# Sinkhorn-sorted attention with a maxout layer: values of items 2 and 3 sorted as a row pair, a hand-written order of scores and sorts, and item 4's keys and queries loaded into the values' raw buffer

## The chip, the cores and the metric

The kernel runs on one core of a Trainium2 chip. The metric is device time in microseconds (us) of one execution; the profile takes one execution apart. Engines: PE (TensorE matmul) and PEld (its weight loads), DVE (VectorE), ACT (ScalarE), POOL (GpSimd, which here issues the loads) and SP (SyncE, which issues output DMAs and DMA transposes).

## The reference, cut to what matters

Four items (B = 4), 8 heads, 768 positions in 8 blocks of 96, head size 64. Each head's 8 x 8 sort matrix is normalised five times, and mixes the blocks of keys and values; attention then stays within a block. The result goes through a maxout layer.

```python
P = sort_net
for _ in range(5):
    P = exp(P - max(P)); P = P / sum(P, -1); P = P / sum(P, -2)
k_sorted = einsum('bhij,bhjcd->bhicd', P, k_blocks)
v_sorted = einsum('bhij,bhjcd->bhicd', P, v_blocks)
attn = softmax(q_blocks @ k_sorted.T / sqrt(64))          # per block, 96 x 96
x = (attn @ v_sorted) as [B * S, H * D] = [3072, 512]
out = maximum(x @ w1, x @ w2) @ w_out                     # 512 -> 1024 -> 512
```

The kernel takes max(a, b) as relu(a - b) + b, so it needs w1 - w2 (`w_difference`) and the product w2 @ w_out (`w_product`, from `w2_transposes`).

## The kernel before, in words

The items are called 1 to 4 here; in the code they are b = 0 to 3. All matrix operands are bf16, converted from f32 by the loads.

**Stages.** A prelude computes the sort matrices and item 1's attention. Then comes `for b in range(B)`: loop 1 (b = 0) does the layer of item 1 and the attention of item 2 between its parts, loop 2 the layer of item 2 and the attention of item 3, loop 3 that of items 3 and 4, and loop 4 only the layer of item 4. A loop's layer is a list `units`: eight `moe_h` (four hidden-column tiles for each half of the tokens, eight matmuls each), in loop 1 then four `w_product`, then twelve `moe_out` parts (six 128-token tiles, two parts of six matmuls each). Loop 1's first two `moe_h` are done in the prelude. After each unit some attention steps are emitted.

**Attention steps of an item.** `sort_k` (three calls of 32 matmuls) mixes keys; `sort_v` (four calls of 16) or `sort_v_pair` (eight calls of 16, for two items at once) mixes values; `q_transposes` (two halves) turns queries; `scores` (eight, SC[u]) multiplies and takes the exponential on ACT; `values` (eight, VA[u]) multiplies by the sorted values and normalises on DVE with a reciprocal and a product; `x_transposes` (four, TR[t]) turns the result, on PE for item 1 and by DMA transposes from SP's queue for the others. Queries of items 1 and 2 are turned on PE, those of items 3 and 4 by `pair_q` (two DVE copies) and a DMA transpose on SP.

**Which half of the array.** Values lie in `v_raw`, 128 partitions: rows 0 to 63 for one item (heads x blocks), rows 64 to 127 for another. `turn_v` reorders them into `v_dc`. A sort of values contracts over 64 rows: `sort_v` uses one half of PE's rows, `sort_v_pair` puts one item on each half by turns. Before, item 1 is in the first half, item 2 in the second, and items 3 and 4 share the buffer as a pair. `block_diagonals` builds the sort matrices' block-diagonal operands from the `selections`.

**What sets the order.** Each engine runs its instructions in program order (`manual_schedule`). Steps are placed in two ways before the change: `tail`, a dictionary from a unit's number to steps, and `steps`, a list that is spread evenly over the units from unit `lo` on:

```python
steps += group(*SC[0:2]) + VA[0:1] + group(*SC[2:4]) + VA[1:2] + group(VA[2], TR[0])
steps += group(*SC[4:6]) + VA[3:4] + group(VA[4], TR[1]) + group(*SC[6:8]) + VA[5:6]
...
want = -(-len(steps) * sum(cost[lo : n + 1]) // total)
```

So scores come in pairs. Copies out of PSUM (`evac`) go to ACT or DVE by `pick`, which compares two running counts of work, `load`; `elapse` lowers them. PSUM holds four tiles of 128 x 1024 f32 (`ps_f32`, `ps_bf16`); an `out_ps` tile is held over four `moe_out` parts.

**Loads.** All go through POOL's queue, in order: `load_k` in three pieces, `load_v` in two (item 1: three), `load_q` in one (item 1: four). Raw keys have two buffers, raw queries one (`q_raw`), raw values the one `v_raw`, so a load waits until the buffer's last reader is done. `keep_streaming` puts matmuls of zeros on PE in the prelude.

Of the kernel before, what the change touches and what calls it, by code (L numbers as in the profile page):

```python
# [16 lines left out]
def kernel(  # L17
# [114 lines left out]
    def load_q(b, by_pair=False):  # L132
        t = qpool.tile([128, H, R * D], BF16, tag="q_raw", name="q_raw", bufs=1)
        src = q[b].rearrange("h (p r) d -> p h (r d)", r=R)
        for hs in [slice(hp, H, HP) for hp in range(HP)] if by_pair else [slice(0, H)]:
            nc.gpsimd.dma_start(out=t[:, hs], in_=src[:, hs])  # L136
        q_raw[b] = t
# [7 lines left out]
    def load_k(b):  # L145
        k_raw[b] = kpool.tile([128, HB * D], BF16, tag="k_raw", name="k_raw")
        n = HB * D // NCH
        for ci in range(NCH):
            nc.gpsimd.dma_start(
                out=k_raw[b][:, ci * n : (ci + 1) * n],  # L150
                in_=k_src[b, :, ci * n : (ci + 1) * n],
            )

    def load_v(b, c0=0, pieces=2):
        r0 = (b % 2) * 64
        n = (BLK - c0) * D // pieces
        for m in range(pieces):
            nc.gpsimd.dma_start(
                out=v_raw[r0 : r0 + 64, c0 * D + m * n : c0 * D + (m + 1) * n],
                in_=v_src[b, :, c0 * D + m * n : c0 * D + (m + 1) * n],  # L160
            )
# [18 lines left out]
    load_v(0, 0, 3)  # L180
# [24 lines left out]
    load_v(1)  # L205
# [48 lines left out]
    maskJ = const.tile([128, 6, NB], FP32, tag="maskJ", name="maskJ")  # L254
# [26 lines left out]
    def selections(b):  # L281
        src = ident[0:G, b * 8 : b * 8 + 8]
        if b % 2 == 0:
            sel_v[b] = const.tile([G, 16, NB], BF16, tag=f"sel_v{b}", name="sel_v")
            nc.vector.tensor_copy(
                out=sel_v[b], in_=ident[0:G, b * 8 : b * 8 + 16].to_broadcast([G, 16, NB])
            )
        sel_k[b] = const.tile([G, 8, 16], BF16, tag=f"sel_k{b}", name="sel_k")
        nc.vector.tensor_copy(out=sel_k[b], in_=src.to_broadcast([G, 8, 16]))
# [3 lines left out]
    def block_diagonals(kinds, m0=0):  # L293
# [3 lines left out]
        for c, (m, b) in enumerate(kinds):  # L297
            sel = (
                sel_k[b].rearrange("g h w -> g (h w)")
                if m  # L300
                else sel_v[b].rearrange("g h j -> g (h j)")
            )
            nc.tensor.matmul(
                pe[:, c * 64 : c * 64 + 64],
                sel,
                p_bf.rearrange("p i j -> p (i j)"),
                start=True,
                stop=True,
            )
# [9 lines left out]
        for c, (m, b) in reversed(list(enumerate(kinds))):  # L319
            bd = const.tile([128, 8, NB], BF16, tag=f"bd{m}{b}", name="bd")  # L320
            nc.vector.tensor_tensor(
                out=bd,
                in0=maskM[:, m].to_broadcast([128, 8, NB]),
                in1=pt[:, c].to_broadcast([128, NB, 8]).transpose([0, 2, 1]),
                op=ALU.mult,
            )
            if m:
                bd_k[b] = bd.rearrange("p m i -> p (m i)")
            else:
                bd_v[b] = bd_v[b + 1] = bd.rearrange("p m i -> p (m i)")  # L330
# [18 lines left out]
    def q_transposes(b, half, eng=None):  # L349
# [11 lines left out]
        if b == 0:  # L361
            nc.tensor.matmul(
                ps[:, 0:128], fill[:, 0:128], ident, is_transpose=True, start=True, stop=True
            )
# [44 lines left out]
    def sort_v(b, t, n=0, eng=None):  # L409
# [3 lines left out]
        for m in range(16):  # L413
# [10 lines left out]
            ps[0:BLK].rearrange("p (d m) -> p m d", m=64),  # L424
            1024,
# [240 lines left out]
    keep_streaming(ps_f32("fill_ps"), 88 * 138, most=138)  # L666
# [15 lines left out]
    sort_k(0, 0, 2048, "A")  # L682
# [7 lines left out]
    SC[0]()  # L690
    SC[1]()
    q_transposes(0, 1, "D")
    SC[4]()
    VA[0]()
    scores(0, 2, 1024)
    VA[1]()
    SC[3]()
    values(0, 2, 1024)
    x_transposes(0, 0, "A")
    values(0, 3, 512)  # L700
# [3 lines left out]
    VA[4]()  # L704
    SC[6]()
    moe_h(0, 0, 0, "A", (1, 3))
    SC[7]()
    VA[5]()
    moe_h(0, 0, 1, "A")
    x_transposes(0, 2, "A")  # L710
    VA[6]()
    w_difference(2)
    VA[7]()
    w2_transposes(0, "D")()
    w_difference(3)
    for b in range(1, B):
        selections(b)
    for c, n, m in [(2, 1, 0), (3, 3, 1)]:
# [9 lines left out]
    def load_rest():  # L728
        load_q(1)
        load_k(2)  # L730

    tail = {
        2: [TR[3], lambda: w2_transposes(1, "A")(), load_rest],
        4: [lambda: turn(second, 0)],
        5: [lambda: block_diagonals([(0, 2), (1, 1), (1, 2), (1, 3)], 2)],
        6: [lambda: turn(second, 24), lambda: turn(second, 48)],
        7: [lambda: turn(second, 72)],
        8: [lambda t=t: sort_k(1, t) for t in range(3)],
        9: [lambda: load_v(2), lambda: load_v(3), lambda: load_k(3)],
        14: [lambda: load_q(2)],  # L740
        18: [lambda: pair_q(2, 0), lambda: pair_q(2, 1), lambda: load_q(3)],
    }
    for b in range(B):
# [20 lines left out]
        steps, lo = [], 0  # L764
        if b < B - 1:
            qs = [lambda half=half: q_transposes(b + 1, half) for half in range(2)]
            ks = [lambda t=t, b=b: sort_k(b + 1, t) for t in range(3)]
            SC, VA, TR = att(b + 1)

            def group(*fs):  # L770
                return [lambda: [f() for f in fs]]

            if b == 0:
                lo = 9
                vs = [lambda t=t: sort_v(1, t) for t in range(4)]
                for m, c in enumerate((0, 24, 48, 72)):
                    VA[m + 1 : m + 2] = group(VA[m + 1], lambda c=c: turn(both, c))
                steps = group(*vs[0:2]) + group(vs[2], qs[0]) + group(vs[3], qs[1])
            elif b == 1:
                vs = [lambda t=t: sort_v_pair(2, t) for t in range(8)]  # L780
                tail[0] = qs
                tail[10] = [lambda: pair_q(3, 0), lambda: pair_q(3, 1)]
                steps = group(*ks) + group(*vs[0:2]) + group(*vs[2:4]) + group(*vs[4:6])
                steps += group(*vs[6:8])
            else:
                tail[0] = qs
                lo = 4
                steps = group(*ks)
            steps += group(*SC[0:2]) + VA[0:1] + group(*SC[2:4]) + VA[1:2] + group(VA[2], TR[0])
            steps += group(*SC[4:6]) + VA[3:4] + group(VA[4], TR[1]) + group(*SC[6:8]) + VA[5:6]  # L790
            steps += group(VA[6], TR[2]) + group(VA[7], TR[3])
        done = 0
        for n, unit in enumerate(units):
            elapse(100 * cost[n] if n < len(cost) else 0)
            unit()
            for step in tail.get(n, []):
                elapse(250)
                step()
            total = sum(cost[lo:])
            want = -(-len(steps) * sum(cost[lo : n + 1]) // total)  # L800
            while done < min(want, len(steps)):
                elapse(250)
                steps[done]()
                done += 1
        tail = {}
# [28 lines left out]
```

## Time and profile before

| | |
|---|---|
| median of 9 runs | 170.4 us (170.01 to 171.63) |
| the profiled execution | 170.89 us, of which the span of the profile is 169.0 us |
| granted PE clock | 1.000 |
| DMA | 23.11 MB moved, 25.17 MB read from HBM |
| scores (32 exponentials) | 24.2 us of ACT |
| values (32 reciprocals and products) | 28.5 us of DVE |
| copies of sorted values | 8 on ACT at 1005 ns, 8 on DVE at 1216 ns |
| matmuls of zeros, 512 columns | 2 in the last two sort matrix steps (6 each), 10 later in the prelude |

The span runs from the first to the last instruction of the program, and the rest of the execution's time lies around it. A busy PE counts the matmuls' own overlap, so the chain of waits (start, length, what) tells better what PE's time goes to: each piece there is the time to the next piece. "issue" in it is time in which an engine waited for nothing that the profile shows.

### The profile page before, as it was taken

To read this page: it belongs to the slowest core of one execution; us is meant where nothing else is said; L and a number is where in the kernel's file an instruction comes from. 1 tells how busy PE (TensorE), PEld (TensorE's weight loads), DVE (VectorE), ACT (ScalarE), POOL (GpSimd) and SP (SyncE) were. 2 spreads that over 40 slices of the span, in tenths; PEclk is the share of its full clock that TensorE was granted. 3 is DMA by queue.
4 is the path that set the end of the run, shared out by engine and by line. 5 is a ranking of instruction groups with operands and counts; after the bars stand their busy time and mean duration, and the time that the engine had idled before them with its cause. 6 is when DMAs were issued, how large, how long until landed. Compare 5 with 4: busy or idle time off the path is not lost.

```text
span 169.0 us, 4544 instructions
## 1 busy us (share of the span) xinstructions
PE 162.6 (96%) x2018; PEld 97.5 (58%) x2018; DVE 75.9 (45%) x174; ACT 85.7 (51%) x104; POOL 28.5 (17%) x44
## 2 busy tenths in 40 slices
PE   7999999999999999999899999999999999999991
PEld 7949666655764454566564545557545456654451
DVE  5978774957454458537643443205442160000011
ACT  4587878465673354176575505456615416642020
POOL 7865585232302004000000000000000000000000
PEclk9999999999999999999999999999999999999999
DMA  3999999999999994999700253590054255000333
GB/s 48 204 205 198 200 207 207 219 204 205 219 212 205 205 234 73 195 158 213 159 0 4 64 153 132 97 291 15 0 36 139 47 176 171 0 0 0 124 142 110
DMA packets 30243, 23.11 MB, mean 137 GB/s; under 512 B 16720, under 2 KB 25168, under 8 KB 30224
## 3 DMA queue, kind: packets, MB, share of 16 engines
q0 software_dynamic: 10880, 12.59, 44.4%
q1 hardware_dynamic: 19200, 10.17, 25.4%
q8 instruction: 16, 0.26, 0.6%
q10 hardware_dynamic: 144, 0.07, 0.1%
q14 instruction: 3, 0.02, 0.0%
HBM read 25.17 MB, written 6.29 MB: 186 GB/s over the span
## 4 chain that ended last, share of the span: by engine, by line
PE 87%; DVE 7%; issue 2%; ACT 2%; DMA 1%
PE out_ps L617 36%; PE h_ps L590 25%; PE o_ps L488 4%; PE wc_ps L570 4%; PE s_ps L461 4%; PE k_ps L394 4%; PE v_ps L415 2%; PE tq_ps L369 2%; PE v_ps L436 1%; DMA p_sb<-in_sort_net_dram 1%; PE tx_ps L526 1%; DVE colsum L243 1%; DVE p_sb L240 1%; ACT v_sb L108 1%; DVE rowsum L239 1%
## 5 line engine op out<-in xcount | busy, mean ns | idle before, releaser
L617 PE MATMUL out_ps<-wo_sb,g 128*128 128x512 bf16 (+2 forms) x200 | 48.5, 371 | 0.2 <-DVE x L505 0.2
L590 PE MATMUL h_ps<-xT,w_sb 128*128 128x384 bf16 x256 | 44.7, 327 | 0.6 <-ACT xT L108 0.4
L590 PEld LDWEIGHTS <-w_sb 128*128 128x128 bf16 x256 | 24.0, 98 | 16.4 <-DVE w_sb L194 0.4
L108 ACT COPY o<-out_ps 128x1024 f32<-128x1024 f32 x11 | 11.1, 1012 | 40.4 <-issue 22.8
L604 ACT ACTIVATE g<-h_ps 128x768 bf16<-128x768 f32 x27 | 21.9, 811 | 17.0 <-PE h_ps L590 17.0
L469 ACT ACTIVATE e<-s_ps 96x768 bf16<-96x768 f32 x32 | 24.2, 804 | 6.4 <-PE s_ps L461 6.4
L617 PEld LDWEIGHTS <-g 128*128 128x128 bf16 x200 | 16.9, 98 | 15.7 <-DVE x L505 0.4
L617 PE MATMUL out_ps<-wc,xT 128*128 128x512 bf16 (+2 forms) x100 | 24.8, 371 | 0.0
L505 DVE TENSOR_TENSOR x<-o_ps,rs 96x512 bf16<-96x512 f32 x32 | 22.0, 686 | 1.1
L499 DVE RECIPROCAL rs<-o_ps 96x8 f32<-96x8 f32 x32 | 6.5, 202 | 34.1 <-PE o_ps L488 34.0
L617 PEld LDWEIGHTS <-xT 128*128 128x128 bf16 x100 | 9.6, 97 | 11.2
L488 PEld LDWEIGHTS <-e 96*128 96x128 bf16 x256 | 11.7, 98 | 6.0 <-ACT e L469 0.2
L488 PE MATMUL o_ps<-v_sb,e 96*128 96x65 bf16 x256 | 12.9, 194 | 0.0
L652 DVE COPY o<-out_ps 128x512 f32<-128x512 f32 (+1 forms) x2 | 1.2, 625 | 25.0 <-PE out_ps L617 25.0
L110 DVE CAST kT<-k_ps 128x1024 bf16<-128x1024 f32 x5 | 6.0, 1223 | 12.3 <-PE k_ps L394 12.3
L110 DVE CAST v_sb<-v_ps 96x1024 bf16<-96x1024 f32 x8 | 9.6, 1216 | 3.1 <-PE v_ps L415 1.7
L461 PEld LDWEIGHTS <-kT 64*128 64x128 bf16 x256 | 6.1, 94 | 6.4 <-issue 5.6
L108 ACT CAST v_sb<-v_ps 96x1024 bf16<-96x1024 f32 x8 | 8.0, 1005 | 3.3 <-PE v_ps L415 1.9
L136 POOL DMA_DIRECT2D q_raw<-in_q_dram x7 | 6.4, 935 | 19.0 <-DVE rs L499 14.0
L461 PE MATMUL s_ps<-qT,kT 64*128 64x96 bf16 x256 | 8.9, 204 | 0.3 <-issue 0.2
L82 PEld LDWEIGHTS <-fill 128*128 128x128 bf16 x98 | 8.0, 117 | 1.6 <-DVE fill L73 1.2
L82 PE MATMUL fill_ps<-fill 128*128 128x138 bf16 x88 | 7.4, 264 | 1.2 <-DVE fill L73 1.2
(77 smaller groups left out, 138.1 us busy)
## 6 DMA issues: line engine op xcount, KB each, us to landing
out_dram<-o SPq DMA_DIRECT2D x11, 512.0 KB, 3.0
k_raw<-in_k_dram POOLq DMA_DIRECT2D x12, 256.0 KB, 12.2
v_raw<-in_v_dram POOLq DMA_DIRECT2D x6, 384.0 KB, 12.7
q_raw<-in_q_dram POOLq DMA_DIRECT2D x3, 768.0 KB, 11.8
w_sb<-in_moe_w_dram POOLq DMA_DIRECT2D x4, 256.0 KB, 9.8
w_sb<-in_moe_w_dram POOLq DMA_DIRECT2D x2, 512.0 KB, 11.2
wo_sb<-in_moe_w_out_dram POOLq DMA_DIRECT2D x2, 512.0 KB, 14.7
v_raw<-in_v_dram POOLq DMA_DIRECT2D x3, 256.0 KB, 4.8
```

The lines of the kernel that those rows point to most:

```text
L82: nc.tensor.matmul(ps[:, 0:w], w0, fill[:, 0:w], start=True, stop=True)
L108: nc.scalar.copy(out=out_ap, in_=in_ap)
L110: nc.vector.tensor_copy(out=out_ap, in_=in_ap)
L394: nc.tensor.matmul(ps[r0 : r0 + 64, m * 64 : (m + 1) * 64], kv[r0 : r0 + 64, t * 16 + m, :], bd_k[b][r0 : r0 + 64, :], start=True, stop=True,)
L461: nc.tensor.matmul(ps[:, h2 * 512 + ii * 128 : h2 * 512 + ii * 128 + BLK], kT[b][rows, (hp * 8 + i) * BLK : (hp * 8 + i) * BLK + 128], rhs ...
L469: nc.scalar.activation(out=e[:, 0 : 8 * BLK].rearrange("p (t c r) -> p t c r", t=8, r=R), in_=ps[0:BLK] .rearrange("p (t f) -> p t f", t=8 ...
L488: nc.tensor.matmul(ps[:, h2 * 512 + ii * 65 : h2 * 512 + (ii + 1) * 65], e[:, (h2 * 4 + ii) * BLK : (h2 * 4 + ii) * BLK + 128], v_sb[:, m0 ...
L505: nc.vector.tensor_tensor(out=x, in0=ov[:, :, :, 0:D], in1=rs.to_broadcast([BLK, 2, 4, D]), op=ALU.mult,)
L570: nc.tensor.matmul(ps[:, 0:512], w2T[:, fb, dmt * 128 : (dmt + 1) * 128], wo_sb[:, fb, :], start=(fb == 0), stop=(fb == NFB - 1),)
L590: nc.tensor.matmul(h_ps[t][:, m * 512 : m * 512 + TCH], w1_sb[:, hp, fb * 128 : (fb + 1) * 128], xT[:, b % 2, ch, hp % 2, hp // 2, :], sta ...
L604: nc.scalar.activation(out=g, in_=src, func=AF.Relu)
L617: nc.tensor.matmul(dst, g_tiles[b, ch, m // 2][:, m % 2, off : off + 128] if m < NFB else xT[:, b % 2, ch, hp % 2, hp // 2, off : off + 12 ...
```

## The change

- **Pairing of values.** Item 2's values go to rows 64 to 127 and item 3's to rows 0 to 63, and both are sorted in loop 1 by `sort_v_pair(2, t)`. Item 4's values are loaded twice, into both halves, and a new `sort_v_halved` (four calls of 16) takes columns 0 to 31 of each head from the first half and 32 to 63 from the second. `selections` makes a selector with two heads' items for b = 0, 2 and 3; `maskJ` has a seventh part and `block_diagonals` makes five kinds in loop 1.
- **Loads.** `load_v(1)` leaves the place before `load_k(1)`; queries of item 2, then values of items 2 and 3 piece by piece, then keys of item 3 follow the prelude. Item 3's queries load into the `w2` buffer after the second `w2_transposes`. Item 4's keys load into the first half of the columns of `v_raw` and its queries into the second, at the end of loop 2's unit 12.
- **Order.** `tails` names for each unit the steps that follow it; the spread list is gone. Scores come in groups of one to three, the pair sort in two threes and a two.
- **Prelude.** Fewer matmuls of zeros, scores 4 ahead of scores 1, one dummy transpose less, `w_difference(2)` ahead of values 7.

The core of the diff:

```diff
     def load_q(b, by_pair=False):
-        t = qpool.tile([128, H, R * D], BF16, tag="q_raw", name="q_raw", bufs=1)
+        if b == 2:
+            t = w2_sb.rearrange("p t f -> p (t f)")[:, 0 : H * R * D].rearrange(
+                "p (h x) -> p h x", h=H
+            )
+        elif b == 3:
+            t = v_raw[:, HB * D :].rearrange("p (h x) -> p h x", h=H)
+        else:
+            t = qpool.tile([128, H, R * D], BF16, tag="q_raw", name="q_raw", bufs=1)
...
     def load_k(b):
-        k_raw[b] = kpool.tile([128, HB * D], BF16, tag="k_raw", name="k_raw")
+        k_raw[b] = (
+            kpool.tile([128, HB * D], BF16, tag="k_raw", name="k_raw")
+            if b < 3
+            else v_raw[:, 0 : HB * D]
+        )
...
-    load_v(1)
     load_k(1)
...
+    def sort_v_halved(b, t, eng=None):
+        m0 = (b % 2) * 64
+        ps = ps_f32("v_ps")
+        for m in range(8):
+            for par in range(2):
+                rows = slice(par * 64, par * 64 + 64)
+                nc.tensor.matmul(
+                    ps[:, par * 512 + m * 64 : par * 512 + (m + 1) * 64],
+                    v_weights(rows, par * 32 + t * 8 + m),
+                    bd_v[b][rows, :],
+                    start=True,
+                    stop=True,
+                )
+        evac(
+            v_sb[:, m0 : m0 + 64, 0:D].rearrange("p m (par d) -> p par m d", par=2)[
+                :, :, :, t * 8 : (t + 1) * 8
+            ],
+            ps[0:BLK].rearrange("p (par d m) -> p par m d", par=2, m=64),
+            1024,
+            eng=eng,
+        )
...
-    sort_k(0, 0, 2048, "A")
+    sort_k(0, 0, 1024, "A")
...
     SC[0]()
+    SC[4]()
+    q_transposes(0, 1, "D")
     SC[1]()
-    q_transposes(0, 1, "D")
-    SC[4]()
     VA[0]()
-    scores(0, 2, 1024)
-    VA[1]()
+    SC[2]()
+    values(0, 1, 512)
     SC[3]()
-    values(0, 2, 1024)
+    values(0, 2, 512)
     x_transposes(0, 0, "A")
-    values(0, 3, 512)
+    VA[3]()
+    VA[4]()
     SC[5]()
...
+    load_q(1)
+    for piece in range(2):
+        for b in (1, 2):
+            load_v(b, which=piece)
+    load_k(2)
...
+    first_tail = {
+        2: [lambda: x_transposes(0, 3)],
+        3: [lambda: w2_transposes(1, "A")(), lambda: load_q(2)],
+        5: [lambda: block_diagonals([(0, 2), (0, 3), (1, 1), (1, 2), (1, 3)], 2)],
+        7: KS,
+        9: [TQ[0], TURN[0]],
+        10: [SC[0], TQ[1], TURN[1]],
+        11: SC[1:4] + TURN[2:4] + [lambda half=half: load_v(3, half=half) for half in range(2)],
+        12: VS[0:3],
+        13: VS[3:6],
+        14: VS[6:8] + [SC[4]],
+        15: [VA[0], lambda: pair_q(2, 0)],
+        16: [VA[1], lambda: pair_q(2, 1)],
+        17: SC[5:8] + [TR[0]],
+        18: [VA[2]],
+        19: [VA[3], TR[1]],
+        20: [VA[4]],
+        21: [VA[5], TR[2]],
+        22: [VA[6], VA[7], TR[3]],
+    }
+    second_tail = {
+        0: [lambda: q_transposes(2, 0), lambda: q_transposes(2, 1)],
+        2: KS,
+        4: SC[0:2],
+        5: [VA[0]],
+        6: SC[2:4],
+        7: [VA[1], TR[0]],
+        8: [VA[2], TURN[0]],
+        9: [VA[3], TR[1], TURN[1]],
+        10: SC[4:7],
+        11: [VA[4], TURN[2]],
+        12: [VA[5], TR[2], TURN[3], lambda: load_k(3), lambda: load_q(3)],
+        13: [VA[6]],
+        14: SC[7:8] + VS[0:2],
+        15: [VA[7], TR[3]],
+        16: VS[2:4],
+        17: [lambda: pair_q(3, 0)],
+        18: [lambda: pair_q(3, 1)],
+    }
+    third_tail = {
+        0: [lambda: q_transposes(3, 0), lambda: q_transposes(3, 1)],
+        2: KS,
+        5: SC[0:2],
+        6: [VA[0]],
+        7: [VA[1], TR[0]],
+        8: SC[2:5],
+        9: [VA[2]],
+        10: [VA[3], TR[1]],
+        11: [VA[4]],
+        12: SC[5:8],
+        13: [VA[5], TR[2]],
+        14: [VA[6]],
+        16: [VA[7], TR[3]],
+    }
...
-            total = sum(cost[lo:])
-            want = -(-len(steps) * sum(cost[lo : n + 1]) // total)
-            while done < min(want, len(steps)):
-                elapse(250)
-                steps[done]()
-                done += 1
```

## The prediction

> **What bounds the kernel now.** I read the page's busy line and clock row first, then a table of windows by stage, then the chain of waits in order of time, last the DMA issues. Items are 1 to 4 here (b = 0 to 3 in the code); loop 1 is the stretch b = 0, and so on.
>
> ```profile
> PE 162.6 (96%) x2018; PEld 97.5 (58%) x2018; DVE 75.9 (45%) x174; ACT 85.7 (51%) x104; POOL 28.5 (17%) x44
> ...
> PEclk9999999999999999999999999999999999999999
> ```
>
> ```profile
> 11.40:30.40 19.00, 17.99 (x407) 13.38 (x406) 13.75 (x26) 14.76 (x18) 12.12 (x15) 1.00 1.32 204
> 30.40:72.30 41.90, 41.65 (x516) 23.98 (x517) 25.49 (x49) 21.00 (x24) 7.46 (x11) 1.00 1.04 196
> 72.30:107.50 35.20, 34.77 (x489) 19.75 (x488) 16.84 (x26) 18.44 (x22) 0.00 (x0) 1.00 0.59 109
> 107.50:139.50 32.00, 31.92 (x361) 17.91 (x360) 10.34 (x19) 15.31 (x19) 0.00 (x0) 1.00 0.43 100
> ```
>
> The windows are the prelude (item 1's attention) and loops 1 to 3; after the window come the length and the busy time of PE, PEld, DVE, ACT and POOL, then clock, DMA share and GB/s. In each loop PE is idle under 0.5 us, at full clock. So the time is PE's list of work, and a change is worth what it takes off that list or adds as waits. The second resource is the loads: 204 and 196 GB/s up to 60 us.
>
> ```profile
> 76.84 0.58 PE v_ps L436 x32
> 77.42 1.41 PE h_ps L590 x8
> 78.82 0.57 PE v_ps L436 x32
> 79.40 1.41 PE h_ps L590 x8
> 80.81 0.54 PE v_ps L436 x30
> 81.35 0.43 issue
> 81.78 0.21 PE v_ps L436 x2
> ...
> 88.53 0.24 PE o_ps L488 x8
> 88.77 1.30 PE out_ps L617 x6
> 90.07 0.45 PE s_ps L461 x16
> 90.52 1.40 PE out_ps L617 x6
> ```
>
> This chain gives prices. Six output matmuls take 1.30 us after a values block (o_ps) but 1.40 after scores; eight h_ps take 1.41 after a sort and 1.30 among themselves. A scores call alone after full-array work takes 0.28, two take 0.45, so one costs 0.17 and entering 0.11. **A visit to a half-array form costs 0.21 us: 0.11 in, 0.10 out**, however many calls it holds.
>
> **The change, part by part.**
>
> *Visits (gain 0.74).* I count 0.105 per switch. Loop 1 before: pe, keys, twice values sort plus query transposes (a third switch each), four score pairs: 18 switches. After: pe, keys, queries, SC0 with queries (a third), SC1-3, two triples of sorts, two sorts with SC4 (same form), SC5-7: 19. Loop 2 before: keys, four sort pairs, four score pairs: 18; after: keys, three score groups, SC7 with two sorts, two sorts: 12. Loop 3: 10 before, 8 after. 46 becomes 39: 7 x 0.105 = 0.74.
>
> *Sorts (gain 0.94).* Item 2's sort was 64 matmuls on one half of the array: 48 took 1.51 us with 0.10 for the switch, 29.4 ns each. A pair's 32 take 0.58 with the switch, 14.8 ns each. Loop 1 changes 64 single for 128 paired: 64 x 29.4 = 128 x 14.8 = 1.9, no gain. Loop 2 changes 128 paired for 64: 64 x 14.8 = 0.94. A rule speaks otherwise: the Trainium skill ("TensorE: Matmul & The Clock Gate", section "Wait — 56ns, not 53.3ns?") has matmul starts never closer than about 25 ns. By it the pair gains almost nothing over single: loop 1 would get 128 x 25 - 1.9 = 1.3 us longer, loop 2 1.6 shorter, 0.3 in all. The rows at 14.8 ns are of these very instructions, so I take 0.94.
>
> *Copies of sorts.* Loop 1 has eight instead of four, loop 2 four instead of eight (1.01 on ACT, 1.22 on DVE); four 64-row turns (0.82 each) leave loop 1's DVE and four 128-row turns move to loop 2. Hidden: DVE is busy 25 of 42 and 17 of 35 us there, ACT 21 and 18; uncovered, four copies are 4.5 us of two engines, 2.2 of PE. The extra selection, mask and fifth block diagonal are some 0.8 us of DVE before the keys' sort; hidden by units 2 to 6 (PE 9 us).
>
> *Prelude (gain 0.6, from 0 to 1.2).* Fills of 512 columns go from ten to five. The two ahead of the first key sort gain nothing: that sort waits for its block diagonal (DVE until about 12.35 us; it started at 12.46). The other three are 3 x 0.22 = 0.65; a dummy transpose (0.16) and one switch (0.1) go too. w_difference(2) moves ahead of the last values block on DVE (0.85 us earlier), which ends the 0.25 idle before h_ps at 30.39. Against that, scores 2 needs the second query copy (0.96 on DVE after 0.79 of transposes); the two fills before it (0.43) were filling that wait, and x_transposes(0, 0) will wait some 0.15 more for its x. 0.65 + 0.16 + 0.1 + 0.25 - 0.43 - 0.15 = 0.6. Waits here were at most 0.36 with the clock at 1.00; mine are about 0.5, so I charge no clock.
>
> *New waits (cost 0.65).* PSUM has four buffers, and an open out_ps holds one for four units. By the durations of the rows (exponential 0.71 to the next, copies 1.0 to 1.2) PE asks too early in four places: the out block after SC1-3 (0.2), the third sort of the first triple (0.2), SC7 of item 2 (0.1), the second sort after SC7 in loop 2, whose buffer waits for DVE's turn and values 6 (0.4). 0.9 in all; the 0.25 wait of out_ps for x at 66.2, behind a turn and two pair_q copies, goes. The 0.43 "issue" pause inside a sort has no shown cause; I leave it. Bounds: gain 0.5 (that pause goes, groups cost nothing) to cost 1.5.
>
> *Loads.* POOL's queue is in order. An item's array is 768 KB, 3.85 us at 204 GB/s. load_v(1) leaves the front of load_k(1), and load_q(1), the four value pieces, load_k(2), load_q(2) follow. wo landed at 16.82 + 15.8 = 32.6; so item 2's keys land at 36.5 (their sort would start at 39), queries 40.3 (44), values 48.0 (the last turns have until 51.8), item 3's keys 51.9, queries 55.7 (pair_q at 60). All hidden, by 2 us at least; each us beyond that would be one of PE. load_q(2) waits on POOL for the second w2 transposes (32 us, long past when its turn comes), and only load_v(3) stands behind it. Item 4's values go twice into 64 rows: the skill's "DMA: Bandwidth & Descriptors" ("Rules for kernel authors") advises against two transfers to disjoint halves since they serialize. By that the pair costs 7.7 us of queue, by one whole transfer 3.85; but queue time runs until 64 us and the turn needs it at 88, so the sum is the same.
>
> Sum: -0.74 - 0.94 - 0.60 + 0.65 = -1.63. The profiled execution took 170.89 (span 169.0 and 1.9 around it), so 169.26; the median of the runs lies 0.49 below it: **168.8 us**.
>
> **The rivals.**
>
> *Item 4's queries late (slower).* Its queries may load only after the last turn of loop 2 (unit 12), and what follows is a line: load, two pair_q on DVE, transpose on SP, scores in unit 5 of loop 3.
>
> ```profile
> q_raw<-in_q_dram POOLq DMA_DIRECT2D x1, 768.0 KB, 11.8
> ```
>
> ```profile
> qT<-q_pair SPq DMA_TRANSPOSE x1, 4.3
> ```
>
> ```profile
> 40.29 0.56 POOL L158 DMA_DIRECT2D v_raw<-in_v_dram  x1 [2.15 <-DVE v_dc L217]
> 41.78 0.52 POOL L158 DMA_DIRECT2D v_raw<-in_v_dram  x1 [0.93 <-DVE v_dc L217]
> ```
>
> The first row is the DMA issues at 65.8 us (issue to landing, among outputs and transposes), the second those at 109. Time there is: from the end of unit 11's matmuls to the scores, PE has 1.78 (unit 12, values 4 and 5), seven units 9.1, values 6 and 7 0.48, SC7 and four sorts 1.53, the wait 0.4, then six units 7.8 and keys 1.74: 22.8. DVE ends the last turn 4.6 after the same point (0.17, out copy 1.14 by the kernel's own load count, values 0.85, turn 0.77, values 0.85, turn 0.82). 18.2 are left; needed are 0.3 + 11.8 + 1.1 + 4.3 = 17.5. That fits by 0.7 only if the keys went ahead, released by the first two turns alone. The third fence speaks for it: load_v(3)'s first piece went 0.3 after the second turn, without the fourth. If the release is of the whole buffer, three key pieces stand ahead on POOL: 3.72 more, late by 3.0: 171.8. It decides from a landing 12.8 us after the last turn; from 14.4 the gain is gone. What lies behind pair_q on DVE is only item 4's key copies, behind the transpose on SP item 4's x transposes. 0.15.
>
> *Item 3's queries late.* Scores 0 of item 3 move from 12.8 to 8.3 us after loop 2's start (five units, keys); the transpose can issue 2.0 after it, behind an output. The one at 74.7 took 7.8, at 109.3 only 4.3. With 7.8 PE waits 2.0 + 7.8 - 8.3 = 1.5: 170.3. Against it: the query load that filled the queues at 66 to 77 us is gone from there. 0.07.
>
> *Groups fill ACT.* Three exponentials take 2.2 us; where an output copy (1.01) comes ahead of them, PE would wait some 0.4. At two of the five triples, 0.8: 169.6. ACT's idle (51% busy) speaks against. 0.15.
>
> **How the numbers follow.** Main case 0.60 at 168.8 (alone 167.6 to 169.6); groups 0.15 at 169.6, item 3's queries 0.07 at 170.3, item 4's queries 0.15 at 171.8, some other delay 0.03. About 0.3% (0.5 us) is what a measurement can tell from no change: faster 0.60 + 0.15 and a small part of the rest 0.76, same 0.07, slower 0.17. The range takes the low end with prelude 1.2 and no new waits, 167.2, and leaves out most of the slow case: to 171.0.
>
> **What would show it.** Right: windows of loops 1 to 3 near 42.2, 34.0 and 31.8; PE v_ps of item 4 as four calls in two visits of about 0.58; five 512-column fills. Wrong: an issue pause before s_ps in unit 5 of loop 3 with a qT transpose that just landed (item 4's queries), or in unit 4 of loop 2; PE waits on exponentials at each triple; a first key load of item 4 after the last turn; h_ps at 30 us no earlier.

## The result, and the profile after

| | before | after |
|---|---|---|
| median | 170.6 us (53 runs, 169.96 to 171.73) | 168.87 us (16 runs, 168.46 to 170.4) |
| ratio after / before | | 0.9912, 95% interval 0.9895 to 0.9929 |
| profiled execution (span) | 170.89 us (169.0) | 168.47 us (166.7) |

The changed kernel is 0.9% faster. Its profiled execution is one of its best, and that of the kernel before is 0.3 us above its median, so the two traces differ by more (2.3 us of span) than the medians (1.7 us). A ratio leaves out every run that took over 1.5% longer than the fastest of its kernel, so that below a ratio and a median can stand apart.

The page of the kernel after, busy time and clock; DVE has more to do, PE still 96%, at full clock:

```profile
PE 159.8 (96%) x2011; PEld 96.5 (58%) x2011; DVE 79.3 (48%) x182; ACT 83.1 (50%) x101; POOL 29.5 (18%) x46
...
PEclk9999999999999999999999999999999999999999
```

The windows of the kernel after (prelude, loops 1 to 3; columns as before):

```profile
11.40:30.00 18.60, 16.73 (x401) 13.13 (x401) 14.46 (x27) 14.81 (x18) 11.86 (x14) 1.00 1.32 202
30.00:72.20 42.20, 42.07 (x583) 24.11 (x581) 26.50 (x52) 20.97 (x25) 5.64 (x10) 1.00 0.98 193
72.20:105.60 33.40, 33.21 (x426) 18.87 (x424) 17.60 (x28) 15.68 (x19) 3.35 (x4) 1.00 0.77 139
105.60:137.30 31.70, 31.70 (x363) 17.99 (x361) 11.30 (x21) 15.52 (x19) 0.00 (x0) 1.00 0.58 112
```

The windows' edges are rounded. Cut at the first matmul of a stage (key sort; third `moe_h` tile; first `moe_h` of each item), the stages are:

| stage | before | after | difference | predicted length |
|---|---|---|---|---|
| key sort to third tile (prelude) | 17.94 | 17.33 | -0.61 | 17.3 |
| loop 1 | 41.95 | 42.20 | +0.25 | 42.2 |
| loop 2 | 35.19 | 33.40 | -1.79 | 34.0 |
| loop 3 | 32.01 | 31.64 | -0.37 | 31.8 |
| loop 4 | 26.13 | 26.13 | 0 | - |

The chain of the kernel after, in loops 2 and 3, shows the same prices as before: groups of three scores (24 matmuls), 1.41 after a half-array form, 1.30 between full-array work, and item 4's sort in 16 matmuls at 0.41 and 32 at 0.57:

```profile
90.36 0.62 PE s_ps L498 x24
90.98 1.41 PE out_ps L654 x6
...
97.70 0.41 PE v_ps L450 x16
98.11 1.40 PE out_ps L654 x6
...
99.76 1.30 PE out_ps L654 x6
101.06 0.57 PE v_ps L450 x32
```

In loop 1 the chain leaves PE once: the third sort of the first triple (v_ps) starts when the exponentials (e) of the three scores ahead of it have ended. A group of three scores takes 0.72 there, where it takes 0.62 above:

```profile
51.35 1.52 ACT e L506 x2
...
52.91 0.41 PE v_ps L473 x16
...
62.15 0.72 PE s_ps L498 x24
```

Where PE still waits after the start, from the kernel after's list of waits (in total, times, longest); only the v_ps one lies behind 30 us. The list has no wait under 0.15 us, so those of loop 1 are not in it:

```profile
PE s_ps L498 <- DVE qT L110: 0.4, 1, 0.4
PE k_ps L408 <- DVE bd L335: 0.4, 1, 0.4
PE o_ps L82 <- PE s_ps L498: 0.3, 1, 0.3
PE h_ps L627 <- ACT xT L108: 0.3, 1, 0.3
PE v_ps L450 <- DVE x L542: 0.2, 1, 0.2
PE tx_ps L563 <- DVE x L542: 0.2, 1, 0.2
```

And the line that the slower rival spoke of, from the timeline of the kernel after (L227 is a turn, L160 a key load of item 4, L143 its query load, L357 `pair_q`, L369 the transpose, L498 the first scores of item 4):

```profile
88.41 0.83 DVE L227 COPY v_dc<-v_raw 128x768 uint32<-128x768 uint32 x1
89.53 1.40 POOL L160 DMA_DIRECT2D v_raw<-in_k_dram  x1 [37.52 <-DVE rs L536]
...
95.98 0.83 DVE L227 COPY v_dc<-v_raw 128x768 uint32<-128x768 uint32 x1
...
97.11 0.89 POOL L143 DMA_DIRECT2D v_raw<-in_q_dram  x1 [4.94 <-DVE rs L536]
...
106.67 1.03 DVE L357 COPY q_pair<-v_raw 128x1536 bf16<-128x1536 bf16 x2 [3.71 <-DMA v_raw<-in_q_dram]
107.73 3.99 SPq L369 DMA_TRANSPOSE qT<-q_pair  x2
115.09 0.51 PE L498 MATMUL s_ps<-qT,kT 64*128 64x96 bf16 x16
```

The first piece of the keys went right behind the first turn, the others (91.1 and 91.6) behind the second, all long before the last turn (95.98 to 96.81); the queries went right behind that. By the landing times of the trace the queries landed at 106.65 and the first half of their transpose, all that the first scores need, at 112.54, 2.6 us ahead of these. Some of the traces below have less to spare.

### The profile page after: what moved, and what is told of

It is laid out like the page before. It is cut to its first block, busy times and chain, and to the rows that moved or that the text cites. A ratio compares the mean times of both kernels' runs of the same rounds, so it can differ in the third digit from the quotient of the medians.

```text
span 166.7 us, 4555 instructions
## 1 busy us (share of the span) xinstructions
PE 159.8 (96%) x2011; PEld 96.5 (58%) x2011; DVE 79.3 (48%) x182; ACT 83.1 (50%) x101; POOL 29.5 (18%) x46
## 4 chain that ended last, share of the span: by engine, by line
PE 83%; DVE 8%; ACT 3%; issue 2%; DMA 1%; ACTq 0%
PE out_ps L654 35%; PE h_ps L627 25%; PE wc_ps L607 4%; PE k_ps L408 4%; PE o_ps L525 4%; PE s_ps L498 3%; PE tq_ps L383 2%; DVE x L542 1%; PE v_ps L473 1%; PE tw_ps L588 1%; ACT e L506 1%; DVE v_dc L227 1%; PE v_ps L429 1%; ACT xT L108 1%; DMA p_sb<-in_sort_net_dram 1%
## 5 line engine op out<-in xcount | busy, mean ns | idle before, releaser
L108 ACT COPY o<-out_ps 128x1024 f32<-128x1024 f32 x9 | 9.1, 1012 | 28.3 <-PE out_ps L654 25.7
L110 DVE CAST kT<-k_ps 128x1024 bf16<-128x1024 f32 x6 | 7.2, 1221 | 7.9 <-PE k_ps L408 7.9
L643 DVE TENSOR_SCALAR g<-h_ps 128x768 bf16<-128x768 f32 x5 | 4.8, 956 | 11.9 <-PE h_ps L627 11.9
L160 POOL DMA_DIRECT2D v_raw<-in_k_dram x3 | 2.5, 823 | 37.7 <-DVE rs L536 37.5
L498 PE MATMUL s_ps<-qT,kT 64*128 64x96 bf16 x256 | 8.7, 204 | 0.4 <-DVE qT L110 0.4
L498 PEld LDWEIGHTS <-kT 64*128 64x128 bf16 x256 | 6.0, 94 | 5.3 <-issue 2.2
```

Source lines behind the costliest of these rows:

```text
L108: nc.scalar.copy(out=out_ap, in_=in_ap)
L110: nc.vector.tensor_copy(out=out_ap, in_=in_ap)
L498: nc.tensor.matmul(ps[:, h2 * 512 + ii * 128 : h2 * 512 + ii * 128 + BLK], kT[b][rows, (hp * 8 + i) * BLK : (hp * 8 + i) * BLK + 128], rhs ...
```

## The experiments

Each was timed beside the kernel before. Loop and prelude lengths are of the profiled runs, cut as in the table above.

**Control: the changed kernel again.** No edit.

> The changed kernel once more, unaltered, so that the three kernels beside it are compared with it on the same chip. Every theory: 1.4 to 2.0 us faster than before (a ratio near 0.991), loops 1 to 3 near 42.2, 33.4 and 31.7 us in the profile.

168.62 us (7 runs, 168.44 to 170.62), ratio 0.9914 (0.9881 to 0.9946). The profiled run was the longest one, 170.62: loops 1 and 3 have the lengths of the table, but the prelude is 19.24 (+1.91) and loop 2 33.68 (+0.28). In loop 2 the first scores of item 3 waited for their transposed queries, which landed at 82.42. The control's list of waits has this line, and the kernel after's has not:

```profile
PE s_ps L498 <- DMA qT<-q_pair: 0.2, 1, 0.2
```

In the prelude the chain shows a pause of PE of 0.89 us where the kernel after has 0.33. First the kernel after:

```profile
20.17 0.33 issue
20.49 0.39 PE o_ps L82
```

and the control:

```profile
20.16 0.89 issue
21.04 0.39 PE o_ps L82
```

Behind it the clock record stands at one half from 22.76 to 26.17 us: ahead of that a stretch of equal length in which PE is busy only 1.91 us. Windows of the control, with PE alone (window, length, busy time, clock, DMA share, GB/s):

```profile
19.34:22.76 3.42, 1.91 (x37) 1.00 1.31 203
22.76:26.17 3.41, 3.41 (x37) 0.50 1.24 208
```

What this pause is, is the question of the second half of the experiments.

**One half.** Item 4 is sorted from one half of the array.

```diff
-    VS = [lambda t=t: sort_v_halved(3, t) for t in range(4)]
+    VS = [lambda t=t: sort_v(3, t) for t in range(4)]
```

> The changed kernel, but item 4's values are sorted on one half of the array: 64 matmuls of 64 columns without a partner, in the same four calls, with the same copies. My theory (a matmul costs 14.8 ns with a partner on the other half and 29.4 ns without): 64 x 14.6 = 0.93 us longer, all of it in loop 2, each visit of two calls 1.04 instead of 0.57 us. By the rule of a floor of 25 ns between matmul starts: 64 x (29.4 - 25) = 0.3 us. If copies out of PSUM set the pace of the sorts: no change.

169.16 us, ratio 0.9931 (0.9915 to 0.9947). Loop 2 is 34.10 instead of 33.40, +0.70, all other stages the same. Its chain has the two groups of 32 matmuls at 1.07 and 1.04, about 32 ns each:

```profile
97.30 1.07 PE v_ps L429 x32
...
101.31 1.04 PE v_ps L429 x32
```

The second of these visits has no wait in either kernel: 1.04 against 0.57, 0.47 us for 32 matmuls, and so 0.94 for all 64. The first loses less, 0.23, mostly because the wait of 0.19 (v_ps for x, in the list above) that stands in it in the kernel after is gone. The floor of about 25 ns between matmul starts, which the prediction took from the Trainium skill ("TensorE: Matmul & The Clock Gate", section "Wait — 56ns, not 53.3ns?") and by which the loss would be some 0.3, does not hold for two matmuls on different halves of the rows: 32 of them take 0.57 us, 0.10 of it for the change of form, which is 14.7 ns each.

**The old prelude.** The prelude's order and zeros are those of the kernel before, the loops those after.

```diff
-    sort_k(0, 0, 1024, "A")
+    sort_k(0, 0, 2048, "A")
...
-    w2T_ready = w2_transposes(0, "D")
+    w2_transposes(0, "D")()
     w_difference(3)
-    w2T_ready()
```

> The changed kernel with the prelude's step order and zero matmuls of before (ten of 512 columns, the dummy transpose, scores 4 after scores 1, the weight difference after values 6). My theory: the prelude is worth about what the two chains show, h_ps of the third tile at 30.39 against 30.02, so 0.4 us longer (0.6 in my prediction), and the loops stay as they are. Rival, that the loops only follow the loads and so an earlier prelude buys nothing: no change in the total.

170.36 us, ratio 1.0002 (0.9983 to 1.0021): the whole gain is gone, not a quarter of it. The prelude from the key sort on is 18.10 (+0.77), and loop 1 43.14 (+0.94); the rest of the loss is a key sort that started at 13.0 instead of 12.5, which other kernels with an unaltered beginning do too in some runs. The loss in loop 1 has one place, in the timeline of this experiment:

```profile
31.81 1.21 DVE L110 COPY w2T<-tw_ps 128x2048 bf16<-128x2048 bf16 x1
...
32.95 0.68 DVE L205 TENSOR_TENSOR w_sb<-w_sb 128x1024 bf16<-128x1024 bf16 x1
...
33.68 1.47 PE L627 MATMUL h_ps<-xT,w_sb 128*128 128x384 bf16 x8 [0.75 <-DVE w_sb L205]
```

Unit 3's h_ps waits for `w_difference(3)`, which stands behind the copy of the turned w2. In the kernel before, the second `w2_transposes` (0.9 us of PE) stood between units 2 and 3 and covered that; the new loop has moved it behind unit 3. So the new loop needs the new order on DVE.

**The copy first.** This order alone.

```diff
-    w_difference(3)
-    w2T_ready()
+    w2T_ready()
+    w_difference(3)
```

> The changed kernel with two steps of the prelude exchanged: the copy of the turned w2 goes ahead of w_difference(3) on DVE, as it does in the kernel before; the whole computation is done. Theory (w_difference(3) is what unit 3 of loop 1 waits for, and this order with the second w2 transposes moved behind that unit is where putting the old prelude back lost its 0.94 us in loop 1): h_ps waits about 0.9 us for w_sb, loop 1 43.1 instead of 42.2, time 169.8 (ratio 0.997). Rival (the loss came from the old order of scores and values in the prelude): loop 1 stays at 42.2, 168.8.

The list of the change above does not name this exchange, but the change makes it.

169.01 us, ratio 0.9907 (0.9879 to 0.9934), which can't be told from the control. The trace can: loop 1 is 42.65, +0.45, with h_ps waiting 0.28 us for w_sb. About half of the 0.94: the old prelude also has `values` 6 behind the second layer tile, which makes all of DVE's line later. That other half was not tried by itself.

**Single scores.** Each group of scores in loops 2 and 3 is taken apart, the later calls one unit later: four visits more in loop 2, five in loop 3.

```diff
-        10: SC[4:7],
-        11: [VA[4], TURN[2]],
-        12: [VA[5], TR[2], TURN[3], ...],
+        10: [SC[4]],
+        11: [VA[4], SC[5], TURN[2]],
+        12: [VA[5], SC[6], TR[2], TURN[3], ...],
```

> The changed kernel with every scores call of loops 2 and 3 that was in a group on its own (scores 7 of item 3 stays with its sorts): 4 more visits in loop 2 and 5 more in loop 3. My theory, 0.21 us a visit: 0.84 and 1.05, 1.9 us longer in all, about as slow as before. Rival, that a switch hides behind PE's queue, or that groups of three cost waits for PSUM that single calls don't: 0 to 0.5 us longer, or shorter.

170.79 us, ratio 1.0014 (0.9989 to 1.0038). Loop 2 34.00 (+0.60) and loop 3 32.85 (+1.21), 1.81 for nine visits, 0.20 each. In loop 2 the wait of 0.19 ahead of the second sort is gone, too; without that help the nine would cost 2.00, 0.22 each. The chain in loop 3 shows the single call at 0.28 and the full-array work behind it at 1.41; a second such pair stands at 118.39, where the kernel after has 0.45 once:

```profile
116.32 0.28 PE s_ps L498 x8
116.60 1.41 PE h_ps L627 x8
```

(In this profiled run, too, the key sort began at 13.0, which makes it 0.5 longer.)

**Keys last.** Item 4's keys and queries exchange their halves of the buffer, so that the keys wait for the last turn as well.

```diff
-        t = v_raw[:, HB * D :].rearrange("p (h x) -> p h x", h=H)
+        t = v_raw[:, 0 : HB * D].rearrange("p (h x) -> p h x", h=H)
...
-            else v_raw[:, 0 : HB * D]
+            else v_raw[:, HB * D :]
```

> The changed kernel with the two halves of item 4's raw buffer exchanged: keys in the later columns, queries in the earlier ones, keys still first in POOL's queue. So the keys can no longer go ahead after the second turn: both loads stand behind the last turn (at 96.8 us). The whole computation is done. Theory (the early release of the keys is what keeps item 4's queries in time): three key pieces take 3.7 us of the queue more after the last turn, the queries land near 110.4 instead of 106.65, their transpose near 116.3 instead of 112.5, and the scores of unit 5 in loop 3, which start at 115.2 and had 2.6 us to spare, wait about 1.1 us; the key sort of item 4 (109.5) is still in time if the keys land 4 to 8 us after issue. Loop 3 32.7 instead of 31.6, time 169.7 (ratio to the kernel before 0.996). With the landing time of the prediction (11.8 us after its issue) it would be 3.0 later: 171.8. Rival (the slack is larger than it looks, loads of such size are hidden either way): 168.6 to 168.9.

172.6 us (5 runs, 170.5 to 173.13), ratio 1.0131 (1.0093 to 1.0169): slower than before. The profiled run is the best of these, with loop 3 at 33.58, +1.94, and everything else unchanged. Its chain:

```profile
98.17 13.74 DMA v_raw<-in_q_dram
...
111.94 1.03 DVE q_pair L357 x2
112.97 1.14 DVE kT L110
...
114.15 2.77 PE h_ps L627 x16
...
117.03 0.52 PE s_ps L498 x16
```

Keys and queries were issued from 95.5 to 99.1, the keys landed at 101.4 to 105.0 and the queries at 111.91, 13.7 after their issue. The rival is real. Its price in this run, 1.94, lies between the 1.1 expected here and the 3.0 of the prediction; three of the other four runs are longer at a mean clock of 0.99, and their part of the price has no trace. But PE hardly waits at the scores (0.10): it waits 1.6 us at the second h_ps tile after the key sort, for DVE's copy of the sorted keys. That copy stands behind the two `pair_q` copies on DVE, which wait for the queries, and its PSUM tile is the one that h_ps needs.

**Long zeros.** 24 matmuls of zeros at the start, instead of 86 (the kernel before has 88 there).

```diff
-    keep_streaming(ps_f32("fill_ps"), 86 * 142, most=142)
+    keep_streaming(ps_f32("fill_ps"), 86 * 142)
```

> The changed kernel with the zero matmuls at the start cut into 24 of up to 512 columns instead of 86 of 142: the same 12,212 columns, 62 matmuls or 124 PE instructions fewer; the whole computation is done. Theory (PE stops where the next 16 KB block of its instructions has not come yet; a block is 256 instructions): every block boundary falls 62 matmuls later in the program. The pause of 0.2 to 0.9 us near 20.2 us (inside item 1's scores) goes, or moves to about 22 us, where the half-rate work gives more time; the prelude gets 0.3 us shorter in a typical run, and the runs near 170.4, in which a long pause is followed by the clock at half for 3.4 us, get rare: 168.4 median, none over 169.5. But a new pause may come up where a boundary now falls into a sort. Rival (the pause belongs to this place, a wait on a semaphore or a buffer that the profile does not show): the pause stays at the second scores after the first values block, 168.6 to 168.9 with a run in four near 170.4.

172.43 us (12 runs, 170.15 to 174.22), ratio 1.0059 (1.0022 to 1.0097). The pause moved, so it doesn't belong to a place; but it came earlier and seven times as long, where I had expected it later or gone; only the last sentence of the theory, on a boundary inside a sort, came true. Chain of the profiled run (174.22):

```profile
16.21 0.98 PE v_ps L429 x30
17.19 2.46 issue
19.66 0.23 PE v_ps L429
```

The clock is at one half from 18.65 to 28.89. The trace's single DMA records explain it. The page has a queue `q8 instruction`, first that of the kernel after, then that of this one (packets, MB, share):

```profile
q8 instruction: 16, 0.26, 0.6%
```

```profile
q8 instruction: 15, 0.25, 0.5%
```

Its packets have 16,384 bytes each. The kernel after has 2011 matmuls, each with a weight load, some 4,020 PE instructions: about one packet for each 251. From the start PE stops after 351 matmuls in the kernels before and after and in the control, and after 223 here, 128 matmuls or 256 instructions earlier: so a packet is taken to be a block of 256. In each case PE goes on 1.3 to 1.4 us after the end of a packet:

| | PE enters the block | packet of the next block | PE stops, goes on |
|---|---|---|---|
| before | 14.71 | 17.87 to 18.84 | 20.07, 20.28 |
| after | 14.91 | 18.12 to 19.09 | 20.17, 20.49 |
| control | 14.92 | 18.72 to 19.68 | 20.16, 21.04 |
| long zeros | 13.40 | 17.42 to 18.39 | 17.19, 19.66 |

From entering a block to the next one 5.6 to 6.3 us pass. From its first matmul to its last this block of sorts and turns takes only 3.6 to 5.2; the later blocks of the kernel after last 6 to 16 us. With 62 matmuls of zeros fewer, the block that ends at 223 began inside the key sort instead of ahead of it, and the sorts ran through it in 3.6 us.

**Short zeros.** The same edit the other way (`most=96`, 128 matmuls), to test that reading with a number given beforehand.

> The changed kernel with the zeros at the start in 128 matmuls of up to 96 columns instead of 86 of 142: the same columns, 42 matmuls more; the whole computation is done. Theory (blocks of 128 matmuls; the next block comes about 5.6 us after PE enters a block, as it did in the kernels before and after): matmul 223 lies in the middle of the key sort, at 13.8 us, and 351 inside the second turn of the queries, reached at 18.1; its block comes at 19.4, so PE stops for 1.3 us inside tq_ps, not after s_ps, and the prelude is 1.0 longer: 169.8; with the clock at half for 3.4 us after so long a pause 171.5. Rival (the pauses are tied to a place or to a wait that the profile does not show, and the long one with long zeros was of those zeros): pause of 0.33 after s_ps as before, 168.7.

172.37 us (13 runs, 169.55 to 173.69), ratio 0.9964 (0.9931 to 0.9997). The chain of the profiled run (172.31):

```profile
17.95 0.36 PE tq_ps L383 x6
18.30 1.16 issue
19.47 0.71 PE tq_ps L383 x18
```

PE stops inside the second turn of the queries, at 18.30 (expected 18.1), for 1.16 us (1.3), and goes on at 19.47 (19.4), after 351 matmuls again, though 42 of them are new. The block is the cause. The clock then stood at one half from 21.07 to 27.90 us. Eight of the 13 runs are at 172.3 or more, all with a mean clock near 0.98.

**Zeros back.** The ten 512-column matmuls of zeros of before, in the new order.

```diff
-    sort_k(0, 0, 1024, "A")
+    sort_k(0, 0, 2048, "A")
...
-    SC[2]()
-    values(0, 1, 512)
+    scores(0, 2, 1024)
+    VA[1]()
...
-    values(0, 2, 512)
+    values(0, 2, 1024)
...
-    VA[3]()
+    values(0, 3, 512)
```

> The changed kernel with the ten 512-column matmuls of zeros of the kernel before in place of five (two more ahead of the key sort, two ahead of scores 2, one more ahead of values 2, one ahead of values 3, one less ahead of values 1); the whole computation is done. Theory (the zeros are worth what the prediction took for them): the two ahead of the key sort cost nothing, the two ahead of scores 2 lie in its wait for the second query copy (0.43), one more costs 0.22 to 0.3: prelude 0.2 to 0.5 longer, 169.2 (ratio 0.993). Rival 1 (they keep the clock up): the run in four at half clock goes, so that the median is that of the good runs, 168.5 to 168.8, and no run is over 169.5. Rival 2 (each zero matmul costs its 0.22 in full): 0.65 to 1.1 longer, 169.7.

168.76 us (5 runs, 168.2 to 168.98), ratio 0.9884 (0.9855 to 0.9913). The prelude from the key sort on is 17.30, against 17.33. Five zero matmuls more cost nothing: they lie in the waits for the query copy, the instruction block and x. So the three times 0.22 that the prediction booked for fewer zeros were no gain beyond the waits that it booked against them.

**Zeros ahead of the stop**, and **fewer zeros**.

```diff
-    SC[2]()
-    values(0, 1, 512)
+    scores(0, 2, 1024)
+    VA[1]()
```

> The changed kernel with the 512 columns of zeros ahead of values 1 in the prelude taken away and 1024 put ahead of scores 2; the whole computation is done. Theory (PE stops after the 16 KB block of its instructions that ends at matmul 351; the next block comes no earlier than about 20.5 us, so what stands ahead of that point is free and what stands behind it costs): the zeros fill the wait for the second query copy (0.43) and the pause (0.33), and the 0.22 of the zeros behind the pause is saved: prelude 0.2 shorter, 168.3 to 168.6 (ratio 0.989), and no run near 170.4, since PE is never idle for long before 20.5 us. Rival (the order of the zeros is of no weight, each costs 0.22): 0.22 longer, 168.9 to 169.1, with a run in four near 170.4.

168.51 us (6 runs, 168.37 to 169.31), ratio 0.9892 (0.9864 to 0.9919). Without the zeros ahead of values 2 and of the first `moe_h` as well:

> The former kernel without the two later matmuls of zeros either (ahead of values 2 and of the first moe_h); the whole computation is done. Theory (zeros behind 20.5 us lie in waits for DVE's x and ACT's xT): nothing to 0.3 shorter, 168.1 to 168.6. Rival (they keep the clock): one more stretch of 3.4 us at half clock in most runs, 170 to 170.5.

168.57 us (9 runs, 168.04 to 170.17), ratio 0.9909 (0.9875 to 0.9943), three of the nine runs at 169.8 or more, with a mean clock of 0.99. And the changed kernel again, beside these:

> The changed kernel, unaltered, beside the three others. Theory and rival alike: 168.5 to 168.9 in most runs, with a run in four near 170.4.

169.01 us (6 runs, 168.44 to 170.07), ratio 0.9919 (0.9888 to 0.9951). `Zeros ahead` is 0.5 us below this second control, as expected, but the intervals overlap by far: that it beats the changed kernel is not shown. The profiled run of `zeros ahead` tells something else. Its instruction block came late, and PE stopped for 0.95 us, longer than in the first control, yet its clock stayed at 1.00, and the prelude of this run is 17.84, longer and not shorter. First its chain, then its window:

```profile
20.36 0.95 issue
```

```profile
17.95:21.37 3.42, 2.38 (x54) 1.00 1.39 200
```

In the control the 0.43 us wait for the query copy lies just ahead of the pause, in the same stretch; here zeros fill that wait.

## Why the prediction was right, step by step

The sum was -1.63 us on the profiled execution, and 168.8; measured are 168.87 and -1.7 between the medians. Between the two profiled executions it is -2.42: there some 0.8 was gained that the sum did not have (a pause of 0.43, 0.2 of waits charged and not met, 0.16 in loop 3). That the medians lie so close to the sum is in part luck; that the large terms, the order of the loops and the sign are right is not.

- **Visits.** Predicted 0.21 us each. Nine added cost 1.81, 0.20 each. Right. Loop 3 gained 0.37 for one visit fewer (0.21); the rest is a wait of the first scores of item 4 in the kernel before, about 0.15, that is gone with them one unit later.
- **Pairing.** Predicted 0.94 in loop 2 and nothing in loop 1. Undone, it costs 0.47 for half of the sorts where no wait stands beside them, and 0.70 in all, with a wait of 0.19 that it hides. Right, the row of the trace against the skill's floor. In loop 1 the matmuls of sorts take 2.34 us (128) instead of 2.07 (64); the 0.27 more is nearly all in a wait of the next step (0.25).
- **New waits.** Predicted 0.9 in four places, and they are in these four places, 0.67 in all. The out block behind SC1-3 starts 0.74 after the triple's start (50.06 to 50.80) where another starts 0.61 after it (90.30 to 90.91): 0.13 (predicted 0.2). The first triple of sorts in loop 1 takes 1.13 us where the second takes 0.88: 0.25 (0.2). The triple with SC7 of item 2 takes 0.72 instead of 0.62: 0.10 (0.1). The second sort behind SC7 in loop 2 waits 0.19 (0.4). So this term was too large by 0.2, all of it in the last place.
- **The 0.43 pause in loop 2.** I left it standing as without a shown cause. It is gone, and this is most of why loop 2 gained 1.79, not 1.2. In the kernel before PE entered the block at 75.1, the packet of the next one came at 79.30 to 80.31, and PE went on at 81.78. That is 893 matmuls and 5 other PE instructions behind the stop in the prelude, seven blocks of 256 instructions to within one. In the kernel after the block of this place (76.3 to 82.3) is no longer, but the packet of the next one, the ninth of the queue in both kernels, had come by 76.64. The load of item 4's queries, under way from 65.81 to 77.56 in the kernel before, is gone from there; whether that, or the order of the loop, let the packet come earlier was not tried alone.
- **Prelude.** Predicted 0.6, measured 0.61, but not by the terms that were booked. Zeros and the waits that they filled were booked at 0.65 - 0.43 - 0.15 = 0.07, and `zeros back` moves the prelude by 0.03: right, and both waits are in the trace, at 0.43 (scores 2) and 0.18 (x). The dummy transpose and the switch (0.26) stand ahead of the stop for the instruction block, where nothing is gained: from the key sort PE goes on behind it after 7.83 us before and 7.96 after. All of the gain is in one late stretch, from the second layer tile to the third: 3.67 us before (26.72 to 30.39), 2.78 after (27.08 to 29.86), for 0.25 booked. There a values block (0.24) has moved to an earlier place, and the wait for `w_difference(2)` is gone; what the other 0.4 is was not separated. I also misread the diff, and the list of the change has it so: `w_difference(2)` stood ahead of values 7 in both kernels. It does start 1.5 us earlier (28.12, was 29.65), since values 6 now go ahead of the second layer tile.
- **"I charge no clock."** Right for the typical run, wrong for some. Four runs of the changed kernel are over 170 us; three of them (170.62, 170.14, 170.07) have a mean clock of 0.99, which one stretch of 3.41 us at one half makes, and the control's trace, of the first of these, has that stretch behind a pause and a wait. The fourth, 170.4, has a mean clock of 0.999, and why it was long is open.
- **Loads.** Item 2's keys and queries and the values of items 2 and 3 were predicted to land at 36.5, 40.3 and 48.0, item 3's keys and queries at 51.9 and 55.7; they landed at 36.30, 41.11, 48.47, 51.57 and 55.39. Item 4's values went twice, one transfer after the other: their four pieces landed 1.8 to 1.9 us apart, the last at 62.75, 7.4 us behind the load ahead of them, where the prediction took 7.7 from the skill's rule.
- **Item 3's queries.** This rival (0.07) is closer than it was given. In the kernel after the first half of their transpose took 5.70 us and landed at 80.16, 0.23 ahead of the scores (80.39). In the control it took 6.07, and in `long zeros` and `short zeros` 6.39 and 6.27; there the scores waited for it, and loop 2 was 0.28, 0.60 and 0.45 longer.
- **Item 4's queries.** They landed 9.84 us after the last turn's end, where the prediction had up to 11.8 from issue and a limit of 12.8. In `fewer zeros`, with the keys ahead as well, they landed 12.35 after it and loop 3 was 0.31 longer, so the limit is some 0.5 lower than predicted. Without the keys ahead they landed at 111.9, 15.1 after the last turn, and loop 3 lost 1.94. The deadline was nearly right, the place of the wait in that run wrong: the prediction named the key copies behind `pair_q` on DVE and did not go on to ask who needs their PSUM tiles.
- **Groups that fill ACT.** One of the five triples of scores makes PE wait for exponentials, for 0.25 and not 0.4: the sort behind SC1-3 (52.91), whose tile is free when the last of them ends.

## What to carry to other kernels

Where PE is the bound, price the visits to a half-array form and count them: here nine were worth 1.8 us. A buffer that is shared by halves is worth more if the first reader to finish frees the half that must be loaded first in its queue; exchanging the halves turned a gain of 0.9% into a loss of 1.3% in the median of its runs. And a step's cover moves with the order: before an edit of a loop is judged alone, look at what the moved step had been hiding (the old prelude under the new loop lost all of the gain).

## What the runs showed of the hardware

- **PE's instructions arrive in blocks, and short matmuls can outrun them.** One DMA packet of 16,384 bytes brings 128 matmuls with their weight loads. With the DMA queues near 200 GB/s, the next block was ready 5.5 to 6.3 us after PE had entered one in the prelude; in loop 2 of the kernel before, at 185 GB/s, it was 6.7. A stretch of 128 matmuls that takes less then ends in a pause that the chain calls "issue": 0.2 to 0.95 us in the kernels with the given start, 2.46 us with a start of 62 matmuls fewer. Where the packet comes early there is no pause: the block of 6.0 us in loop 2 of the kernel after has none. The number of matmuls of zeros at the start, not only their time, so decides where pauses fall.
- **The clock goes by stretches of 3.41 us, and a partly idle one can be enough.** All changes of the clock record lie on a grid of 3.41 us: in the control 17.07 us, five steps, lie between the record's start at 5.69 and the change at 22.76, and the next is at 26.17. While the kernel ran, the half clock followed stretches in which PE was busy for 1.91 (control), 1.87 (`short zeros`), 1.96 (`long zeros`) and 2.46 us (`fewer zeros`); it did not follow 2.38 (`zeros ahead`), 2.42 (`copy first`) and 2.47 (the kernel after), nor any stretch with more, and not 1.96 in loop 3 of `keys last` (110.61 to 114.02) either. So the busy time of a stretch, as the trace models it, does not decide by itself; what does is open. The Trainium skill ("TensorE: Matmul & The Clock Gate", "Part 1: The HAM clock gate") has this free-running window, but puts an idle one ahead of the half clock. Where the grid lies differs from run to run, so the same wait and pause fall into one stretch or into two; with the lateness of the block, that may be what makes the few runs of the changed kernel at a mean clock of 0.99. Only one of these was profiled.
- **Start.** The key sort began between 12.5 and 13.2 us in the profiled runs, with the same beginning of the program in most. Why is open.
